# A hand-ordered first batch is reordered: thirteen exponential buffers, other engines for four casts, a split third hash, another beginning

## The chip, the cores and the metric

The kernel runs on one NeuronCore of a Trainium2 chip. The metric is the device time of one execution in microseconds (us); a lower time is better. One execution is also recorded by the hardware profiler, and its trace gives every instruction's start and length.

## The reference

Two blocks follow each other. Inputs are random normal: q, k, v of shape (4 batches, 8 heads, 768 rows, 64), a projection of 64 x 6, and the weights of a gated feed-forward block.

```python
q_bits = (einsum('bhsd,dk->bhsk', q, proj) > 0)        # 6 sign bits of each row; the same for k
mask   = q_bucket[:, :, :, None] == k_bucket[:, :, None, :]   # all six bits equal
scores = where(mask, q @ k.T / 8, -1e9);  attn = softmax(scores);  attn_out = attn @ v
x = attn_out.transpose(0, 2, 1, 3).reshape(3072, 512)
out = x + sigmoid(x @ w_res) * ((gelu(x @ w_gate) * (x @ w_val)) @ w_out)
```

So attention is restricted to rows that hash to the same of 64 buckets; then each of 3072 tokens goes through a feed-forward block of width 1536.

## The kernel before, in words

**Pairs and chunks.** Two heads make a pair p; a batch has four pairs, 0 to 3, and all four batches sixteen. For a pair, the rows of q (side 0) and k (side 1) lie on 128 partitions in 12 tiles of 128 rows (six of each head). The scores of a pair are cut into nine chunks of 1024 columns. Chunk c of the first batch (0 to 35, four pairs by nine) appears in the order as `('S', c)`: three matmuls into a PSUM tile `sp` (L500) of which there are two, and one exponential on ScalarE (ACT, L510) into a buffer. `('V', c)` is the product of that buffer with the values on TensorE (PE, L475).

**The hash as part of the scores.** A row carries, beside its 64 elements, six entries of plus or minus 0.5 from its sign bits and a constant, so that one matmul over 71 rows gives both the score and a large penalty where the bits differ. To get there: `cast` writes the elements as bf16 into `nat` (there are four `nat` tiles, pair p and side use number (2p+side) mod 4); `tr` transposes the f32 rows in 32x32 blocks on VectorE (DVE, L272) into `t32`; `hash` or `hash1` multiplies that with the projection on PE (L283, L318); `tokens` transposes the result back (L295); `bits` writes the signs (L304, L325); `turn` transposes `nat` on PE (L373) and `copy` takes it out of PSUM into `aug` (L381 on DVE, L379 on ACT), or `turn_dma` does both by a DMA on SP's queue (L360). The scores read `aug`.

**Values and results.** `va` and `vs` (GpSimd, POOL, L386 to L398) prepare the values and a sum over them; `finish` (DVE, L419 and L420) divides by the row sums into `x_tok`, which gets turned into `x_sb` by a DMA on SP's queue for pairs 0 and 1 (L428) and on PE for pairs 2 and 3 (`xturn`, L459, copied by L461 and L464). The feed-forward block of the first batch (L524, `gate_val`) reads `x_sb` and starts when the last pair's is there; before it, three quarters of its first two sums are done by `('gv', 0)` and `('gv', 1)`.

**Order.** Nothing is scheduled automatically: each engine runs its instructions in the order in which the code records them. For the first batch this is the list `PLAN`, entry by entry; `STEP` maps the names to functions. The letters in a step name the engine (`'v'` DVE, `'s'` ACT, `'p'` POOL). An entry's place binds only relative to others of its engine: a `load` is a DMA on SP's queue and is issued when the SP entries before it have been issued and its buffer is free. Buffers come free by use: q and k each have four load buffers, freed by `cast` and `tr` of the pair that held them. From batch 1 on, the order comes from loops that the change does not touch.

**Exponential buffers.** In the first batch the exponentials go round a ring of NE = 9 slots, which lies where `hidden` will be later; in later batches they go round the four buffers of `e_pool`.

Of the kernel before, what the change touches and what calls it, by code (L numbers as in the profile page):

```python
# [10 lines left out]
BF16 = mybir.dt.bfloat16  # L11
# [6 lines left out]
    ('load', 1, 0), ('load', 1, 1), ('load_v', 0), ('load', 2, 0), ('load_v', 1), ('load', 2, 1),  # L18
    ('load', 3, 0), ('proj', 's', 'pssp'), ('proj', 'w', 'pppp'), ('cast', 0, 1, 'p', 0, 6),
# [13 lines left out]
    ('S', 3), ('hash', (1,), 0), ('hash', (1,), 1), ('turn', 0, 1, 6, 12, 'f'), ('hash', (1,), 2),  # L33
    ('copy', 0, 1, 6, 8, 'v'), ('copy', 0, 1, 8, 12, 'v'), ('hash', (1,), 3),
# [5 lines left out]
    ('load', 4, 0),  # L40
    ('S', 8), ('V', 5), ('load_v', 4), ('turn', 1, 0, 6, 12, 'r'), ('copy', 1, 1, 0, 6, 'v'),
    ('finish', 0, 0),
    ('S', 9), ('V', 6), ('V', 7),
    ('S', 10), ('load', 5, 1), ('V', 8),
    ('S', 11), ('tr', 3, 1), ('tr', 2, 1), ('copy', 1, 0, 6, 12, 'v'), ('turn', 1, 1, 6, 12, 'f'),
    ('V', 9), ('finish', 0, 1),
    ('S', 12), ('hash', (2, 3), 0), ('hash', (2, 3), 1), ('va', 3), ('copy', 1, 1, 6, 12, 'v'),
    ('hash', (2, 3), 2), ('hash', (2, 3), 3), ('cast', 3, 1, 'p'),
# [7 lines left out]
    ('turn_dma', 3, 0),  # L56
# [15 lines left out]
    ('S', 34), ('hash', (4, 5), 0), ('finish', 3, 0), ('hash', (4, 5), 1),  # L72
    ('S', 35), ('V', 32), ('hash', (4, 5), 2), ('hash', (4, 5), 3), ('V', 33), ('va', 4),
    ('open', 4, 0), ('V', 34), ('V', 35), ('load', 7, 0), ('load_v', 6), ('tr', 7, 0), ('finish', 3, 1),
# [19 lines left out]
def kernel(  # L94
# [13 lines left out]
    B, H, S, D = q.shape  # L108
# [3 lines left out]
    P = 128  # L112
# [19 lines left out]
    NE = 9  # L132
# [108 lines left out]
    for s in range(3):  # L241
        n = KF // 3
# [166 lines left out]
    av = {}  # L409
# [383 lines left out]
```

## Time and profile before

| | |
|---|---|
| Time, median of 3 runs | 341.53 us (340.52 to 341.78) |
| Span of the profiled execution, first to last instruction | 338.4 us |
| The profiled execution's own time | not listed apart from its span; the median is 3.1 us above the span |
| PE, DVE, ACT, POOL busy | 330.2, 215.4, 214.3, 176.6 us |
| Granted TensorE clock, mean | 1.000 |
| DMA | 43.9 MB, mean 130 GB/s |

A row of the timeline gives the start, the length, the engine, the line of the kernel, the operation with what it writes and reads, and how many instructions are merged into it; in brackets stands how long the engine was idle before, and what ended that. "PEld" are weight loads of PE; an engine's name with a q is its queue. Matmuls are pipelined, so the rows of PE overlap.

### The profile page before, as it was taken

To read this page: it belongs to the slowest core of one execution; us is meant where nothing else is said; L and a number is where in the kernel's file an instruction comes from. 1 tells how busy PE (TensorE), PEld (TensorE's weight loads), DVE (VectorE), ACT (ScalarE), POOL (GpSimd) and SP (SyncE) were. 2 spreads that over 40 slices of the span, in tenths; PEclk is the share of its full clock that TensorE was granted. 3 is DMA by queue.
4 is the path that set the end of the run, shared out by engine and by line. 5 is a ranking of instruction groups with operands and counts; after the bars stand their busy time and mean duration, and the time that the engine had idled before them with its cause. 6 is when DMAs were issued, how large, how long until landed. Compare 5 with 4: busy or idle time off the path is not lost.

```text
span 338.4 us, 7607 instructions
## 1 busy us (share of the span) xinstructions
PE 330.2 (98%) x2995; PEld 203.2 (60%) x3042; DVE 215.4 (64%) x454; ACT 214.3 (63%) x247; POOL 176.6 (52%) x264
## 2 busy tenths in 40 slices
PE   8999999999999999999999999999999999999996
PEld 6676765565666655665666665666565665666444
DVE  7987465655477968877577896876478444343243
ACT  4989962237999962437999982255999984322220
POOL 3798930235289952578799981657979100000000
PEclk9999999999999999999999999999999999999999
DMA  6999999999966333529067932725050360000012
GB/s 216 371 259 177 289 191 152 166 161 227 300 207 158 82 97 82 96 44 188 3 157 231 280 90 85 141 47 93 2 125 33 79 103 31 33 0 2 31 62 97
DMA packets 74388, 43.89 MB, mean 130 GB/s; under 512 B 52544, under 2 KB 71360, under 8 KB 74352
## 3 DMA queue, kind: packets, MB, share of 16 engines
q1 hardware_dynamic: 67872, 37.95, 46.1%
q0 software_dynamic: 6400, 5.44, 10.5%
q8 instruction: 24, 0.39, 0.5%
q14 instruction: 12, 0.10, 0.1%
q10 hardware_dynamic: 80, 0.00, 0.0%
HBM read 29.56 MB, written 6.29 MB: 106 GB/s over the span
## 4 chain that ended last, share of the span: by engine, by line
PE 81%; POOL 8%; ACT 5%; DVE 3%; issue 2%; DMA 1%; POOLq 0%; DVEq 0%; ACTq 0%
PE sp L524 36%; PE fps L570 14%; PE sp L500 13%; PE av L475 7%; PE rps L556 5%; ACT ering L510 5%; POOL pr L335 4%; PE hs L283 3%; PE wps L228 1%; PE hs L318 1%; POOL v L394 1%; PE pt L373 1%; DMA x_sb<-x_tok 1%; DVE sums L341 1%; POOL va L386 1%
## 5 line engine op out<-in xcount | busy, mean ns | idle before, releaser
L335 POOL TENSOR_TENSOR pr<-ld,projr 128x384 f32<-128x384 f32 x96 | 93.8, 998 | 47.8 <-DVE sums L341 31.6
L510 ACT ACTIVATE e<-sp 128x1024 bf16<-128x1024 f32 x108 | 109.0, 1027 | 8.3 <-PE sp L500 3.2
L541 ACT ACTIVATE gt<-sp 128x768 bf16<-128x768 f32 x48 | 38.9, 810 | 82.3 <-PE sp L524 78.6
L500 PE MATMUL sp<-aug,aug 71*128 71x256 bf16 (+1 forms) x384 | 85.9, 325 | 1.2 <-ACT ering L510 0.6
L570 PE MATMUL fps<-wo,hh 128*128 128x512 bf16 (+2 forms) x287 | 74.4, 361 | 1.3
L544 DVE TENSOR_TENSOR hh<-gt,sp 128x768 bf16<-128x768 bf16 x48 | 45.8, 954 | 42.9 <-PE sp L524 39.1
L524 PE MATMUL sp<-x_sb,wg 128*128 128x512 bf16 (+1 forms) x377 | 70.5, 325 | 0.4
L524 PE MATMUL sp<-x_sb,wv 128*128 128x512 bf16 (+1 forms) x374 | 70.4, 324 | 0.5
L341 DVE TENSOR_REDUCE sums<-pr 128x6 f32<-128x384 f32 x96 | 50.2, 542 | 10.7 <-POOL pr L335 10.3
L475 PEld LDWEIGHTS <-e 128*128 128x128 bf16 x864 | 40.2, 97 | 25.1
L524 PEld LDWEIGHTS <-wg 128*128 128x128 bf16 x384 | 37.1, 98 | 25.8 <-issue 1.5
L524 PEld LDWEIGHTS <-wv 128*128 128x128 bf16 x384 | 37.5, 98 | 24.9 <-issue 0.2
L475 PE MATMUL av<-va,e 128*128 128x65 bf16 x864 | 43.4, 193 | 0.2
L570 PEld LDWEIGHTS <-hh 128*128 128x128 bf16 x312 | 28.1, 97 | 21.6
L500 PEld LDWEIGHTS <-aug 71*128 71x128 bf16 x384 | 29.3, 97 | 12.6 <-issue 3.7
L510 ACT ACTIVATE ering<-sp 128x1024 bf16<-128x1024 f32 x36 | 34.2, 1037 | 1.9 <-PE sp L500 1.7
L573 DVE SCALAR_TENSOR_TENSOR fps<-th,fps 128x512 f32<-128x512 f32 (+2 forms) x26 | 17.0, 653 | 25.9 <-PE fps L570 25.8
L556 PE MATMUL rps<-wr,x_sb 128*128 128x512 bf16 x91 | 26.0, 379 | 0.2
L560 ACT ACTIVATE th<-rps 128x512 f32<-128x512 f32 x24 | 14.3, 594 | 18.7 <-PE rps L556 18.5
L272 DVE STREAM_TRANSPOSE t<-ld 128x768 f32<-128x768 f32 (+3 forms) x28 | 23.1, 844 | 2.5 <-PE hs L283 1.9
L454 DVE COPY av<-av 128x390 f32<-128x390 f32 x24 | 13.6, 565 | 14.6 <-PE av L450 14.5
L262 POOL TENSOR_SCALAR nat<-ld 128x768 bf16<-128x768 f32 (+1 forms) x12 | 9.6, 804 | 19.9 <-DMA aug<-nat 16.9
(72 smaller groups left out, 264.4 us busy)
## 6 DMA issues: line engine op xcount, KB each, us to landing
ldv<-in_v_dram SPq DMA_DIRECT2D x16, 384.0 KB, 4.9
out_dram<-o SPq DMA_DIRECT2D x23, 256.0 KB, 2.1
ld<-in_q_dram SPq DMA_DIRECT2D x15, 384.0 KB, 5.1
ld<-in_k_dram SPq DMA_DIRECT2D x15, 384.0 KB, 5.2
wg<-in_moe_w_gate_dram POOLq DMA_DIRECT2D x4, 384.0 KB, 6.3
wv<-in_moe_w_val_dram POOLq DMA_DIRECT2D x4, 384.0 KB, 8.5
wo<-in_moe_w_out_dram POOLq DMA_DIRECT2D x3, 512.0 KB, 7.3
wr<-in_moe_w_res_dram POOLq DMA_DIRECT2D x1, 512.0 KB, 13.8
```

What stands on the lines that cost most here:

```text
L272: nc.vector.transpose(t32[p, side][:, sl].rearrange("p c h n -> p (c h n)"), raw[p, side][:, sl].rearrange("p c d -> p (c d)"))
L335: nc.gpsimd.tensor_mul(pr, raw[x][:, hi * T:(hi + 1) * T], projr[:, bit].unsqueeze(1).to_broadcast([P, T, D]))
L341: nc.vector.reduce_sum(sums[x][:, hi * T:(hi + 1) * T, bit], pr, axis=mybir.AxisListType.X)
L475: nc.tensor.matmul(av[p, hi][:, qt, :], e[:, off:off + P], va[:, hi, jt, 0:D + 1], start=first, stop=(repeats(p, hi) and jt == T - 1), ski ...
L500: nc.tensor.matmul(sp[:, off:off + nq * P], ks[0:KA, hi * T + jt, :], qs[0:KA, hi * T + qt0:hi * T + qt0 + nq, :], start=True, stop=True)
L510: nc.scalar.activation(e, sp, AF.Exp, scale=float(ALPHA))
L524: nc.tensor.matmul(sp[:, c0:c1], w[:, kk, bass.ts(m, P)], xs[:, kk, c0:c1], start=(kk == 0), stop=(kk == KM - 1))
L541: nc.scalar.activation(gt, sp[:, 0:S], AF.Gelu)
L544: nc.vector.tensor_mul(hidden[b][:, m, :], gt, ps[1][:, 0:S])
L556: nc.tensor.matmul(rps, x_sb[b][:, kk, t, :], wr[:, kk, :], start=(kk == 0), stop=(kk == KM - 1))
L570: nc.tensor.matmul(fps[:, cs], hh[:, m, bass.ts(t, P)], wo[:, m, cs], start=(m == 0), stop=(m == KF - 1))
L573: nc.vector.scalar_tensor_tensor(fps[:, cs], th[:, cs], 1.0, fps[:, cs], op0=ALU.add, op1=ALU.mult)
```

## The change

`PLAN` is replaced by another order of almost the same steps (36 S, 36 V, 20 `tr`, 14 `cast`, 15 `copy` in each), and the exponential of chunk c goes to slot c mod 13: slots 0 to 8 are the ring, and 9 to 12 are taken from `e_pool`. What else differs:

- `cast` of (2,1), (4,0), (4,1) and (5,0) is on DVE and no longer on POOL. Of the bits of pairs 2 and 3, DVE writes 11 parts of 16 (5 before).
- The third hash, `('hash', (4, 5), ...)`, has its four parts after chunks 29, 31 and 35 (two); before, after 34 (two) and 35 (two).
- At the beginning, POOL spreads the projection for the four-pair hash (`projw`) ahead of the one for the first pair (`projs`); the small 256-column filler matmul stands just before chunk 0; DVE's last transposition of the first q moves ahead of the first bits; four copies on ACT (three before) come ahead of chunk 0.
- The copy of (0,0) rows 6 to 12 goes from ACT to DVE, that of (0,1) rows 6 to 8 from DVE to ACT.
- The first two weight loads (`('w',)`) are issued on POOL behind `va` of pair 4 and not after chunks 6 and 13.
- SP issues the loads in another order: among them, `load` of (6,1) comes ahead of the first turn of x, and (5,1) behind it.
- The Gelu table is loaded ahead of the last copy of x.

The diff, cut to what the text speaks of:

```diff
-    ('load', 3, 0), ('proj', 's', 'pssp'), ('proj', 'w', 'pppp'), ('cast', 0, 1, 'p', 0, 6),
-    ('cast', 0, 0, 'p', 6, 12), ('tr', 0, 0, 0, 4), ('cast', 0, 0, 's', 0, 6), ('fill', 1, 256),
...
-    ('S', 10), ('load', 5, 1), ('V', 8),
...
-    ('V', 9), ('finish', 0, 1),
...
-    ('S', 15), ('load', 6, 1), ('bits', 3, 0, 'p'), ('V', 12), ('turn', 2, 1, 0, 6, 'f'),
...
-    ('S', 34), ('hash', (4, 5), 0), ('finish', 3, 0), ('hash', (4, 5), 1),
-    ('S', 35), ('V', 32), ('hash', (4, 5), 2), ('hash', (4, 5), 3), ('V', 33), ('va', 4),
+    ('proj', 'w', 'pppp'), ('tr', 0, 0, 0, 4), ('proj', 's', 'pssp'), ('cast', 0, 0, 'p', 6, 12),
+    ('tr', 0, 1, 0, 2), ('fill', 7), ('cast', 0, 0, 'p', 0, 6), ('hash1', 0, 0, 0, 4, 'av'),
+    ('load', 1, 0), ('tr', 0, 1, 2, 6), ('load', 1, 1), ('tr', 0, 0, 4, 6), ('hash1', 0, 1, 0, 2, 'av'),
+    ('cast', 0, 1, 'p', 6, 12), ('tr', 0, 0, 6, 12), ('bits1', 0, 1, 0, 2), ('cast', 0, 1, 's', 0, 6),
...
+    ('fill', 1, 256), ('tr', 1, 1), ('va', 0), ('load', 3, 1), ('load', 4, 0), ('copy', 0, 1, 2, 6, 's'),
+    ('copy', 0, 0, 4, 6, 's'),
+    ('S', 0), ('hash1', 0, 1, 6, 12, 'av'),
+    ('S', 1), ('turn', 0, 0, 6, 12, 'av'), ('bits1', 0, 1, 6, 12),
+    ('S', 2), ('hash', (1,), 2),
+    ('S', 3), ('turn', 0, 1, 6, 12, 'f'), ('hash', (1,), 3), ('copy', 0, 1, 6, 8, 's'), ('hash', (1,), 0),
+    ('vs', 0), ('cast', 2, 0, 'p'), ('tr', 2, 0), ('hash', (1,), 1), ('copy', 0, 0, 6, 12, 'v'),
+    ('tokens', (1,)),
...
+    ('S', 9), ('cast', 3, 0, 'p'), ('copy', 1, 0, 6, 12, 'v'), ('V', 6), ('load_v', 3), ('load', 6, 1),
+    ('S', 10), ('V', 7), ('vs', 1), ('tr', 3, 1), ('tr', 2, 1), ('turn', 1, 1, 6, 12, 'f'),
+    ('finish', 0, 0), ('V', 8), ('cast', 2, 1, 'v'),
+    ('S', 11),
+    ('S', 12), ('finish', 0, 1), ('hash', (2, 3), 0), ('hash', (2, 3), 1), ('hash', (2, 3), 2),
+    ('copy', 1, 1, 6, 12, 'v'), ('hash', (2, 3), 3), ('tokens', (2, 3)),
+    ('S', 13), ('bits', 2, 0, 'vvvp'), ('bits', 2, 1, 'vvvp'), ('V', 9), ('cast', 3, 1, 'p'),
...
+    ('S', 17), ('V', 14), ('copy', 2, 1, 0, 6, 'v'), ('load', 5, 1), ('copy', 2, 0, 0, 6, 'v'),
...
+    ('S', 19), ('va', 2), ('tr', 5, 1), ('copy', 2, 0, 6, 12, 'v'), ('finish', 1, 0), ('V', 15),
+    ('V', 16),
+    ('S', 20), ('copy', 2, 1, 6, 12, 'v'), ('V', 17), ('turn_dma', 3, 1),
...
+    ('S', 27), ('V', 24), ('tr', 5, 0), ('va', 4), ('V', 25), ('w',),
+    ('S', 28), ('V', 26),
+    ('S', 29), ('hash', (4, 5), 2), ('cast', 4, 1, 'v'), ('load_v', 6),
...
+    ('S', 31), ('finish', 2, 1), ('hash', (4, 5), 3),
...
+    ('S', 35), ('hash', (4, 5), 0), ('hash', (4, 5), 1), ('V', 33), ('V', 34), ('w',), ('tr', 7, 0),
+    ('V', 35), ('finish', 3, 1), ('gelu',), ('open', 4, 0), ('tr', 7, 1), ('gv', 0), ('vs', 4),
...
-            e = ring[0][:, (p * NCH + c) % NE]
+            n = (p * NCH + c) % (NE + 4)
+            e = ring[0][:, n] if n < NE else e_pool.tile([P, 1024], BF16, tag="e", name="e")
```

More of the change, by code (lines that the diff above doesn't have):

```diff
@@ L17 @@
 PLAN = [
-    ('load', 1, 0), ('load', 1, 1), ('load_v', 0), ('load', 2, 0), ('load_v', 1), ('load', 2, 1),
-    ('load', 3, 0), ('proj', 's', 'pssp'), ('proj', 'w', 'pppp'), ('cast', 0, 1, 'p', 0, 6),
[13 rows of a table removed]
-    ('S', 3), ('hash', (1,), 0), ('hash', (1,), 1), ('turn', 0, 1, 6, 12, 'f'), ('hash', (1,), 2),
-    ('copy', 0, 1, 6, 8, 'v'), ('copy', 0, 1, 8, 12, 'v'), ('hash', (1,), 3),
[5 rows of a table removed]
-    ('load', 4, 0),
-    ('S', 8), ('V', 5), ('load_v', 4), ('turn', 1, 0, 6, 12, 'r'), ('copy', 1, 1, 0, 6, 'v'),
-    ('finish', 0, 0),
@@ L43 @@
-    ('S', 9), ('V', 6), ('V', 7),
-    ('S', 10), ('load', 5, 1), ('V', 8),
-    ('S', 11), ('tr', 3, 1), ('tr', 2, 1), ('copy', 1, 0, 6, 12, 'v'), ('turn', 1, 1, 6, 12, 'f'),
-    ('V', 9), ('finish', 0, 1),
-    ('S', 12), ('hash', (2, 3), 0), ('hash', (2, 3), 1), ('va', 3), ('copy', 1, 1, 6, 12, 'v'),
-    ('hash', (2, 3), 2), ('hash', (2, 3), 3), ('cast', 3, 1, 'p'),
[7 rows of a table removed]
-    ('turn_dma', 3, 0),
[15 rows of a table removed]
-    ('S', 34), ('hash', (4, 5), 0), ('finish', 3, 0), ('hash', (4, 5), 1),
-    ('S', 35), ('V', 32), ('hash', (4, 5), 2), ('hash', (4, 5), 3), ('V', 33), ('va', 4),
@@ L74 @@
-    ('open', 4, 0), ('V', 34), ('V', 35), ('load', 7, 0), ('load_v', 6), ('tr', 7, 0), ('finish', 3, 1),
-    ('gv', 0), ('tr', 7, 1), ('xturn', 3), ('preset', 4, 0), ('tokens', (4, 5)), ('gv', 1),
-    ('repeat', 4, 0), ('gelu',),
+    ('proj', 'w', 'pppp'), ('tr', 0, 0, 0, 4), ('proj', 's', 'pssp'), ('cast', 0, 0, 'p', 6, 12),
[6 rows of a table added]
+    ('turn', 0, 1, 2, 6, 'f'), ('copy', 0, 0, 0, 4, 's'), ('load_v', 1), ('load', 3, 0),
+    ('bits1', 0, 0, 6, 12), ('tr', 1, 0), ('turn', 0, 0, 4, 6, 'r'), ('cast', 1, 0, 'p'),
@@ new lines @@
+    ('S', 12), ('finish', 0, 1), ('hash', (2, 3), 0), ('hash', (2, 3), 1), ('hash', (2, 3), 2),
+    ('copy', 1, 1, 6, 12, 'v'), ('hash', (2, 3), 3), ('tokens', (2, 3)),
+    ('S', 13), ('bits', 2, 0, 'vvvp'), ('bits', 2, 1, 'vvvp'), ('V', 9), ('cast', 3, 1, 'p'),
[17 rows of a table added]
+    ('S', 29), ('hash', (4, 5), 2), ('cast', 4, 1, 'v'), ('load_v', 6),
+    ('S', 30), ('V', 27), ('V', 28), ('tr', 6, 0), ('cast', 5, 0, 'v'),
+    ('S', 31), ('finish', 2, 1), ('hash', (4, 5), 3),
+    ('S', 32), ('V', 29), ('V', 30),
@@ L77 @@
+    ('S', 33), ('V', 31), ('finish', 3, 0), ('tr', 6, 1), ('load', 7, 1),
+    ('S', 34), ('V', 32), ('xturn', 2),
+    ('S', 35), ('hash', (4, 5), 0), ('hash', (4, 5), 1), ('V', 33), ('V', 34), ('w',), ('tr', 7, 0),
+    ('V', 35), ('finish', 3, 1), ('gelu',), ('open', 4, 0), ('tr', 7, 1), ('gv', 0), ('vs', 4),
+    ('xturn', 3), ('load_v', 5), ('preset', 4, 0), ('tokens', (4, 5)), ('repeat', 4, 0), ('gv', 1),
 ]
```

58 rows, old and new, of the table PLAN are left out of this document.

## The prediction, on record before the change was run

> **What bounds the kernel now.** I read the page first. Its chain of work that ended last gives PE most of the span, and the page's groups of instructions show that one exponential takes about a microsecond on ACT:
>
> ```profile
> PE 81%; POOL 8%; ACT 5%; DVE 3%; issue 2%; DMA 1%; POOLq 0%; DVEq 0%; ACTq 0%
> L510 ACT ACTIVATE ering<-sp 128x1024 bf16<-128x1024 f32 x36 | 34.2, 1037 | 1.9 <-PE sp L500 1.7
> ```
>
> The 81% is an average, and the change lies in the first batch alone. Everything behind it is the same program, bound by PE, so the change is worth exactly as much as it moves the start of the feed-forward block. ACT's timeline from 7 to 50 us shows what sets that start:
>
> ```profile
> 7.07 0.86 ACT L379 ACTIVATE aug<-pt 71x256 bf16<-71x256 bf16 x2 [1.04 <-PE pt L373]
> 8.42 0.38 ACT L379 ACTIVATE aug<-pt 71x256 bf16<-71x256 bf16 x1 [0.50 <-PE pt L373]
> 8.86 3.07 ACT L510 ACTIVATE ering<-sp 128x1024 bf16<-128x1024 f32 x3
> 11.83 0.80 ACT L379 ACTIVATE aug<-pt 71x768 bf16<-71x768 bf16 x1
> 12.52 1.02 ACT L510 ACTIVATE ering<-sp 128x1024 bf16<-128x1024 f32 x1
> 14.02 8.75 ACT L510 ACTIVATE ering<-sp 128x1024 bf16<-128x1024 f32 x9 [0.49 <-PE sp L500]
> 23.73 20.52 ACT L510 ACTIVATE ering<-sp 128x1024 bf16<-128x1024 f32 x22 [0.95 <-PE sp L500]
> 44.49 1.02 ACT L510 ACTIVATE ering<-sp 128x1024 bf16<-128x1024 f32 x1 [0.24 <-PE sp L500]
> 47.86 0.38 ACT L461 ACTIVATE x_sb<-pt 128x256 bf16<-128x256 bf16 x1 [2.35 <-PE av L450]
> ```
>
> The 36 exponentials run nearly without a break: chunk 0 at 8.86, chunk 3 at 12.52, 4 at 14.02, 13 at 23.73, 35 at 44.49. In the chain of waits between 30 and 34 us they are the chain itself, one behind the other:
>
> ```profile
> 31.28 0.80 ACT ering L510
> 32.19 0.81 ACT ering L510
> 33.09 0.82 ACT ering L510
> ```
>
> They start 0.90 to 0.91 apart; I take 0.915 as the free pace. From chunk 0 to 35 that would be 35 x 0.915 = 32.0 us; it took 35.63. So **3.6 us is all that any order can win** if chunk 0 stays where it is. The losses are at chunk 3 and 4 (5.16 - 4 x 0.915 = 1.5), at 5 to 13 (9.71 - 8.2 = 1.5), and little after. The 22 from chunk 13 pace at (20.52 - 1.02) / 21 = 0.929, which puts chunk 22 at 32.1.
>
> **The change, part by part.** I follow when chunks 0, 4, 13, 22 and 35 get their exponential.
>
> *Chunk 0.* Before, the beginning runs so:
>
> ```profile
> 1.07 3.38 PE L228 MATMUL wps<-warm 128*128 128x256 bf16 x8 [1.07 <-POOL warm L191]
> 3.12 0.43 POOL L222 COPY projs<-projn 32x12 f32<-32x12 f32 x2 [1.26 <-DMA projn<-in_proj_dram]
> 3.60 0.87 POOL L222 COPY projw<-projn 32x12 f32<-32x12 f32 x4
> 4.24 1.78 PE L318 MATMUL hs<-t,projs 128*128 128x128 f32 x8
> 5.34 0.33 DVE L323 STREAM_TRANSPOSE hs<-hs 128x128 f32<-128x128 f32 x1 [0.66 <-PE hs L318]
> 5.84 1.07 PE L318 MATMUL wps<-t,projs 128*128 128x128 f32 x8
> 6.45 0.57 DVE L272 STREAM_TRANSPOSE t<-ld 128x384 f32<-128x384 f32 x1
> ```
>
> With projw first, POOL gives projs at 3.12 + 0.87 + 0.43 and a gap, 4.47 for 3.55. The first hash then starts at about 4.7 for 4.24: 0.45 later. DVE's 0.57 of transposition (6.45) moves into its 0.66 of idle time ahead of 5.34 and would win that back, but DVE now takes the second hash's bits first and so waits for both; the turns end about 0.45 later. And ACT has four copies ahead of chunk 0: the new one has the 512 columns that the pair of 0.86 also holds next to a 256 (0.38), so some 0.5, less 0.2 of the 0.50 that ACT idled. Chunk 0: 8.86 + 0.45 + 0.3 = **9.6, 0.75 later**.
>
> *Chunk 4.* How long a chunk takes from the start of its scores on PE to its exponential, where ACT stands idle, chunk 13 shows (exponential at 23.73):
>
> ```profile
> 23.02 0.61 PE L500 MATMUL sp<-aug,aug 71*128 71x256 bf16 x3
> ```
>
> So 0.65 to 0.7. ACT's copy of 768 columns (0.80; it pushed chunk 3 to 12.52) goes to DVE, and a 256-column one (0.38) comes behind chunk 3. Chunks 1 to 3 then follow at the free pace, chunk 3 at 9.6 + 2.75 = 12.35; the copy ends at 13.7, and chunk 4 follows 0.65 later: **14.35, now 0.3 later** than before.
>
> *Chunk 13.* Here PE's whole second hash stood in the way before, and DVE's queue will after:
>
> ```profile
> 21.36 0.54 DVE L381 COPY aug<-pt 71x768 bf16<-71x768 bf16 x1
> 21.59 1.51 PE L283 MATMUL hs<-t,projw 128*32 128x192 f32 x32
> 23.16 0.58 DVE L295 STREAM_TRANSPOSE ht<-hs 128x384 f32<-128x384 f32 x1 [1.26 <-PE hs L283]
> 23.93 3.57 POOL L304 TENSOR_SCALAR nat<-ht 32x72 bf16<-32x72 f32 x7
> 27.87 0.82 POOL L264 CAST nat<-ld 128x768 bf16<-128x768 f32 x1 [0.37 <-POOL nat L304]
> 45.44 0.98 DVE L272 STREAM_TRANSPOSE t<-ld 128x768 f32<-128x768 f32 x1 [1.91 <-PE hs L283]
> ```
>
> The copy at 21.36 is the last that chunk 13 needs. DVE gets there without a pause, now with 0.5 more (the first hash of a whole pair ends later, behind chunk 3) and with the cast of (2,1). No cast on DVE is in the trace. It has 768 elements like the 71x768 copy (0.54) and f32 in SBUF like the transposition of 0.98; I take 0.54, the same operation. The copy ends at 21.9 + 0.5 + 0.54 = 22.95 (23.4 with 0.98), just after the hash (23.0); chunk 13 comes 0.65 later: **23.6, 0.1 earlier** (24.05, 0.3 later, with 0.98).
>
> *Chunk 22* needs two copies of pair 2, and DVE's queue holds `tr` of (5,1) and one `finish` ahead of them. Before, that load was issued at 21.16, long ahead. After, it is on SP behind the turn of x, and its buffer, pair 3's, comes free only with the cast of (3,1): 23.0 + 0.6 (transposition back) + 0.1 + 2 x 0.51 (POOL's bits, 3.57 / 7) + 0.82 = 25.6. How long it then takes, these issues tell: in order the turn of x, the loads issued at 21.16, 23.04, 32.52 and 33.95, and two half loads at the beginning:
>
> ```profile
> x_sb<-x_tok SPq DMA_TRANSPOSE x1, 5.9
> ld<-in_k_dram SPq DMA_DIRECT2D x1, 384.0 KB, 5.6
> ld<-in_k_dram SPq DMA_DIRECT2D x1, 384.0 KB, 8.1
> ld<-in_q_dram SPq DMA_DIRECT2D x1, 384.0 KB, 4.4
> ldv<-in_v_dram SPq DMA_DIRECT2D x1, 384.0 KB, 4.2
> ld<-in_q_dram SPq DMA_DIRECT2D x1, 192.0 KB, 2.4
> 29.42 2.68 DVE L272 STREAM_TRANSPOSE t<-ld 128x768 f32<-128x768 f32 x3
> 32.21 0.56 DVE L420 TENSOR_TENSOR x_tok<-av,rec 128x384 bf16<-128x384 f32 x1
> ```
>
> It has one transfer ahead of it and no weights beside it, so I take 4.2, the row nearest: landing at 29.8, between 28.0 (2.4, half the size, nothing ahead) and 33.7 (8.1). Behind the landing stand 0.9 (2.68 / 3), 0.54, 0.56 and a reciprocal of about 0.2, 0.54, and 0.65 to the exponential, less what neighbours overlap: 3.3. Chunk 22 comes at **33.1 for 32.1, 1.0 later**. At the free pace it would be due at 23.6 + 9 x 0.92 = 31.9, so the wait begins where the load lands after 28.6.
>
> *Chunk 35.* Half of the third hash stood between chunks 34 and 35 (44.49 - 43.23, if 21 paces of 0.929 lead from 23.73 to 43.23, is 1.26, so 0.35 lost); after, the parts lie where PE has room, two behind chunk 35. From 22 to 35: 13 x 0.915 + 0.1 = 12.0 for 12.4. Chunk 35: 33.1 + 12.0 = **45.1, 0.6 later**.
>
> *Behind it* nothing shortens. `tr` of (7,0) waited for the hash at 45.44 and stood ahead of the last `finish`, and does again. The earlier Gelu table saves what the four hash parts beside the first sums cover anyway.
>
> **Priced at nothing.** The thirteen buffers and the allowed lag: by the list, never more than six chunks are issued and not yet multiplied, before (at chunks 5 and 24) and after (at chunk 5), and nine slots hold six; no exponential waits for a slot in either. Three more casts and six more bits on DVE fall where it has pauses (28 to 36 us). The two weight loads issued late:
>
> ```profile
> 40.20 0.84 POOL L247 DMA_DIRECT2D wg<-in_moe_w_gate_dram  x1
> 46.27 1.14 PE L524 MATMUL sp<-x_sb,wg 128*128 128x512 bf16 x6
> wg<-in_moe_w_gate_dram POOLq DMA_DIRECT2D x4, 384.0 KB, 6.3
> ```
>
> They leave POOL behind `va` of pair 4, some three microseconds of casts earlier than 40.2 stood, say 38.5, and land at 44.8, 1.5 ahead of the first use at 46.27. If pair 4's values come two microseconds late, that cover is gone and each one more costs one.
>
> The sum: +0.75 - 0.45 - 0.4 + 1.1 - 0.4 = +0.6 on a span of 338.4, and so on the median of 341.53, which lies 3.1 above the span: **342.1**. A difference of 0.5% (1.7 us) is about what a measurement of this kernel can tell from no change.
>
> [...] POOL's cast takes 0.82 us here and never ran beside a cast on DVE. [...]
>
> **The rivals.**
>
> *The load of (5,1) comes much later (slower; 0.20).* One mechanism: DVE waits at `tr` of (5,1), and what stands behind it are the copies that chunk 22 reads. For it speaks the 8.1 of a load behind a turn of x; against it, that this one shared the DMA engines with a weight load that is moved away. From 31.3 on (5.6) it costs 1.5 more than forecast, at 33.7 it costs 3.9: 343.6 to 346.0.
>
> *PE's slow beginning lasts longer (slower; 0.10).* The eight matmuls of 4.24 took 1.78 us, the eight of the same shapes at 5.84 took 1.07: PE gets faster at about 5.9, after 4.8 us without a pause. After the change it idles between 4.1 and 4.7. If the faster stretch comes only at 9, the hash and turns ahead of chunk 0 cost up to 1.5 more: 343.6. [...]
>
> *The reorder works as such a plan would want (faster; 0.17).* The start is not later than before, since POOL's and ACT's copies overlap better than I let them (-0.75), the load lands by 28.6 (-1.1), and the cast costs less: 340.2, down to 339.5 where PE also closes the gap at chunk 13. Against it speaks that every one of these must hold.
>
> *It does nothing that can be told (forecast's own kind; 0.48).* Between +1.6 and -0.7: 340.8 to 343.1. The rest, 0.05, is weights or values late at 46 us, 344.
>
> **How the numbers follow.** Faster by over 0.5% (below 339.8): most of the faster rival's lower half and a little of its middle, 0.12. Slower by over 0.5% (above 343.2): 0.17 of the load, 0.08 of PE's beginning, 0.04 of the rest, 0.03 of the forecast's upper end, 0.32. Within: 0.56. The range goes from 340.0 (0.13 below it) to 344.6 (the load landing at 32.3; 0.07 above).
>
> **What would show it.** In the changed kernel's ACT timeline, chunk 0 near 9.6, 4 near 14.2, 13 near 23.6, 22 near 33.1 and 35 near 45.1. On DVE, an idle time ended by the DMA of a k load ahead of a transposition near 29 us, with chunk 22's scores waiting behind it. No wait of an exponential for PE's values. The forecast is wrong if chunk 35 starts outside 43.0 to 46.7, or if the distance from chunk 35 to the feed-forward block is not the same as before.

## The result, and the profile after

The changed kernel takes 346.05 us (343.90 to 348.35, six runs) against 340.81 (340.52 to 341.78, six runs of the kernel before on the same chip): 1.0146 times as long, 95% interval 1.0107 to 1.0185. The forecast was 342.1, with a range up to 344.6: the change is slower by more than the range held. The forecast stood on a median of 341.53 and meant 0.6 us more; measured are 5.2 more. (Ratios here leave disturbed executions out, so a ratio can be smaller than the quotient of the medians beside it.)

The profiled execution took 344.31 us, one of the faster of the six, with a span of 342.6 for 338.4. (The kernels' line numbers differ by a few.) The page's chain that ended last now has DMA in it with 6%, where it had 1%:

```profile
PE 78%; POOL 9%; DMA 6%; issue 3%; DVE 3%; ACT 0%; SPq 0%; POOLq 0%; DVEq 0%; ACTq 0%
```

ACT's timeline, in the rows that answer to those of before:

```profile
9.23 3.84 ACT L508 ACTIVATE ering<-sp 128x1024 bf16<-128x1024 f32 x4
12.95 0.38 ACT L376 ACTIVATE aug<-pt 71x256 bf16<-71x256 bf16 x1
13.96 4.83 ACT L508 ACTIVATE ering<-sp 128x1024 bf16<-128x1024 f32 x5 [0.63 <-PE sp L497]
23.50 8.60 ACT L508 ACTIVATE ering<-sp 128x1024 bf16<-128x1024 f32 x9 [0.60 <-PE sp L497]
31.98 3.85 ACT L508 ACTIVATE e<-sp 128x1024 bf16<-128x1024 f32 x4
44.12 1.02 ACT L508 ACTIVATE e<-sp 128x1024 bf16<-128x1024 f32 x1
49.72 0.38 ACT L458 ACTIVATE x_sb<-pt 128x256 bf16<-128x256 bf16 x1 [3.06 <-PE av L447]
```

Up to chunk 35 the change won 0.37 us (44.12 for 44.49). The 36 chunks are not where the time went. POOL's timeline behind them, and PE's first products of x with the weights, show where:

```profile
37.19 0.83 POOL L383 CAST va<-ldv 128x768 bf16<-128x768 f32 x1 [1.49 <-DMA ldv<-in_v_dram]
37.95 0.15 POOL L384 MEMSET va<- 128x12 bf16 x1
42.67 0.99 POOL L244 DMA_DIRECT2D wg<-in_moe_w_gate_dram  x1 [4.57 <-issue]
43.67 0.75 POOL L244 DMA_DIRECT2D wv<-in_moe_w_val_dram  x1
48.20 1.15 PE L522 MATMUL sp<-x_sb,wg 128*128 128x512 bf16 x6 [2.38 <-DMA wg<-in_moe_w_gate_dram]
50.20 1.15 PE L522 MATMUL sp<-x_sb,wv 128*128 128x512 bf16 x5 [0.49 <-DMA wv<-in_moe_w_val_dram]
```

POOL is done with pair 4's values at 38.1, the weight load stands next in its program with no wait of its own, and it leaves 4.57 us later ("issue": nothing that the profile shows was waited for). It lands at 48.16, the second one at 50.16, and PE waits for both. The first exponential of the second batch, chunk 36, stands behind all this; its row before, then after:

```profile
80.74 1.02 ACT L510 ACTIVATE e<-sp 128x1024 bf16<-128x1024 f32 x1
83.19 1.02 ACT L508 ACTIVATE e<-sp 128x1024 bf16<-128x1024 f32 x1
```

It comes **2.44 later**, with chunk 35 0.37 earlier. A second loss of **1.65** follows between chunks 48 and 64 of the second batch (20.05 us for 18.40); from there the distance of 4.1 us stays, and the span ends 4.2 later.

### The profile page after: what moved, and what is told of

It reads as the page before. It is cut to its first block, busy times and chain, and to the rows that moved or that the text cites. A ratio compares the mean times of both kernels' runs of the same rounds, so it can differ in the third digit from the quotient of the medians.

```text
span 342.6 us, 7607 instructions
## 1 busy us (share of the span) xinstructions
PE 330.5 (96%) x2995; PEld 202.0 (59%) x3042; DVE 219.0 (64%) x463; ACT 214.2 (63%) x247; POOL 172.4 (50%) x255
## 4 chain that ended last, share of the span: by engine, by line
PE 78%; POOL 9%; DMA 6%; issue 3%; DVE 3%; ACT 0%; SPq 0%; POOLq 0%; DVEq 0%; ACTq 0%
PE sp L522 36%; PE fps L568 14%; PE sp L497 12%; PE av L472 6%; PE rps L554 5%; POOL pr L332 3%; PE hs L280 2%; DMA wv<-in_moe_w_val_dram 2%; POOL va L383 1%; DMA ld<-in_q_dram 1%; DMA ldv<-in_v_dram 1%; POOL v L391 1%; PE pt L370 1%; PE hs L315 1%; DMA x_sb<-x_tok 1%
## 5 line engine op out<-in xcount | busy, mean ns | idle before, releaser
L508 ACT ACTIVATE e<-sp 128x1024 bf16<-128x1024 f32 x117 | 117.9, 1026 | 10.0 <-PE sp L497 4.8
L472 PEld LDWEIGHTS <-e 128*128 128x128 bf16 x936 | 43.4, 97 | 26.6 <-issue 0.7
L472 PE MATMUL av<-va,e 128*128 128x65 bf16 x936 | 47.0, 193 | 0.2
L508 ACT ACTIVATE ering<-sp 128x1024 bf16<-128x1024 f32 x27 | 25.7, 1026 | 1.3 <-PE sp L497 1.2
L417 DVE TENSOR_TENSOR x_tok<-av,rec 128x384 bf16<-128x384 f32 x32 | 17.8, 557 | 1.1
```

The lines of the kernel that those rows point to most:

```text
L417: nc.vector.tensor_mul(x_tok[b][:, hp, :, hi * D:(hi + 1) * D], o[:, 0:T, 0:D], rec.unsqueeze(2).to_broadcast([P, T, D]))
L472: nc.tensor.matmul(av[p, hi][:, qt, :], e[:, off:off + P], va[:, hi, jt, 0:D + 1], start=first, stop=(repeats(p, hi) and jt == T - 1), ski ...
L508: nc.scalar.activation(e, sp, AF.Exp, scale=float(ALPHA))
```

## What the experiments showed

Theory at the start: the two late weight loads are the whole loss. Rivals: the second batch's loss has another cause; the pause of 4.57 us comes from the new DVE casts beside it, or from transfers in flight, or from POOL's instruction stream. In the diffs, "..." marks lines that are left out, and some lines are cut at their ends.

### 1. The weights early again (e1_w_early)

```diff
-    ('S', 6), ('turn', 1, 0, 0, 6, 'r')
+    ('S', 6), ('w',), ('turn', 1, 0, 0, 6, 'r')
...
-    ('S', 13), ('bits', 2, 0, 'vvvp'), ('bits', 2, 1, 'vvvp'), ('V', 9), ('cast', 3, 1, 'p'),
+    ('S', 13), ('bits', 2, 0, 'vvvp'), ('bits', 2, 1, 'vvvp'), ('V', 9), ('cast', 3, 1, 'p'), ('w',),
...
-    ('S', 27), ('V', 24), ('tr', 5, 0), ('va', 4), ('V', 25), ('w',),
+    ('S', 27), ('V', 24), ('tr', 5, 0), ('va', 4), ('V', 25),
...
-    ('V', 34), ('w',), ('tr', 7, 0),
+    ('V', 34), ('tr', 7, 0),
```

> The changed kernel with its first two weight loads back at chunks 6 and 13, where the kernel before has them; everything else as changed. Theory W (the late weights are the whole loss; 2.44 us at the first product of x with the gate weights, and 1.65 more between chunks 48 and 64 as a consequence of the same lateness): chunk 35 stays near 44.1, chunk 36 comes near 80.4 for 83.2, the 1.65 us behind chunk 48 go too, and the time is 340.4 (340.0 to 341.0). Rival R (the 1.65 us in the second batch have a cause of their own, such as the ring's buffers): 342.1. Rival N (the first products are late for another reason and the weights only show as what came last): 345 to 346.

341.84 us (340.66 to 343.85, ten runs), ratio 1.0043 [1.0018, 1.0068]. Chunk 36 at 80.86 for 83.19: the first loss is the weights'. But 1.3 of the second loss stayed, and the median lies 1.4 above theory W: the late loads are not the whole loss. And chunk 35 came at 44.86, since the second load, issued at 25.32, puts POOL's later work back, and the values of pair 2 are ready 0.7 later, for which PE now waits:

```profile
32.77 0.40 PE L472 MATMUL av<-va,ering 128*128 128x65 bf16 x8 [1.15 <-POOL va L384]
```

### 2. The kernel before with late weights (e2_before_w_late)

```diff
-    ('S', 6), ('w',), ('bits', 1, 1, 'v'),
+    ('S', 6), ('bits', 1, 1, 'v'),
-    ('S', 13), ('cast', 3, 0, 'p'), ('w',), ('tokens', (2, 3)),
+    ('S', 13), ('cast', 3, 0, 'p'), ('tokens', (2, 3)),
-    ('V', 33), ('va', 4),
+    ('V', 33), ('va', 4), ('w',), ('w',),
```

> The kernel before with only its first two weight loads moved from chunks 6 and 13 to behind the values of pair 4 at chunk 35; nothing else changed. Theory W1 (being issued late costs it by itself, since POOL stands idle for some 4.5 us ahead of the first weight load of the group, as in the changed kernel): loads leave at 42 to 43, land at 48, first use about 2 us late, and the other weights later too: 343 to 346. Rival W2 (the 4.5 us of idle time belong to the changed kernel's other transfers, not to the late place): the loads leave at 38.4, land by 43.6 and 45.6, the first use at 46.3 is not late, time 340.8 to 341.8.

342.1 us (340.99 to 345.51, ten runs), 1.0051 [1.0015, 1.0087]. There is no pause, though the loads stand in the same place, right behind the values of pair 4, and are the first that POOL issues:

```profile
40.47 0.16 POOL L387 MEMSET va<- 128x12 bf16 x1
40.51 0.98 POOL L247 DMA_DIRECT2D wg<-in_moe_w_gate_dram  x1
```

They land at 46.22 and 48.14, and the first product comes at 46.58 for 46.27. So late issue alone costs little in this execution, the second fastest of the ten; what makes the 4.57 us is not the late place by itself, which speaks for W2, though the loads left 2 us later than W2 said and the median lies 0.3 above its range. Three of the ten runs, at 344.6 to 345.5, stay unexplained.

### 3. Nine buffers (e3_ring9)

```diff
-            n = (p * NCH + c) % (NE + 4)
-            e = ring[0][:, n] if n < NE else e_pool.tile(...)
+            e = ring[0][:, (p * NCH + c) % NE]
```

> The changed kernel with nine exponential buffers in a ring as before in place of thirteen; the lists stay as changed. Theory: the thirteen buffers do nothing (at most six chunks wait for their values), so the time stays at that of the changed kernel, 346 (344 to 348.5). Rival: the four buffers that it takes from the pool of the later batches, or their order, cost the 1.65 us in the second batch: 344.4 or less. Second rival: the buffers are needed and without them an exponential waits for values: above 348.

346.11 us (345.01 to 346.67, four runs), 1.0152 [1.0120, 1.0185]: the thirteen buffers make no difference that can be told. The pause is there too, 4.82 us, up to 43.01.

This profile shows one more cost of PE's wait. PE waits 2.69 us for the first weight load, and from 49.5 to 52.8 the clock that it is granted is 0.50, where the changed kernel's profile has 1.00. The same six transpositions of x, here (first row) and in the changed kernel:

```profile
49.49 0.85 PE L456 MATMUL pt<-ident,x_tok 128*128 128x128 bf16 x6
49.19 0.50 PE L456 MATMUL pt<-ident,x_tok 128*128 128x128 bf16 x6
```

Chunk 36 comes at 84.59 for 83.19, though the load landed only 0.3 later. In the profile of experiment 6 the clock is 0.50 from 48.4 to 55.1, behind a wait of 1.90; no other profile of these kernels has it below 1.00 before its last 3 us. By these figures such a stretch takes some 1.6 us of PE's work (an estimate: half of 3.3). It fits the runs: the mean granted clock is 0.992 to 0.995 in four of the changed kernel's six, and no run of the kernel before beside the experiments is under 0.997. That the wait brings the lower clock on was not tested by itself.

### 4. The loads a few instructions earlier (e4_w_ahead)

Beside this, the two late places are taken out as in experiment 1.

```diff
-    ('load_v', 4), ('vs', 3),
+    ('load_v', 4), ('vs', 3), ('w',), ('w',),
```

> The changed kernel with its first two weight loads only a few instructions earlier on POOL: behind the sums of pair 3 (about 33.9 us) instead of behind the values of pair 4 (38.1 us). Theory F (POOL's 4.57 us of idle time at 38.1 is a refill of its instruction stream, queued behind loads in flight; it comes at a fixed place in the stream and time, whatever instruction stands there): both loads leave at 34 to 36 without a pause, land by 42, and the pause shows behind them, at the next instructions near 38 to 42: time 340.4 to 342. Theory S (the pause belongs to the first transfer that POOL issues): the pause of some 4.5 us stands ahead of the first weight load, at 34 to 38.5, landing near 44 and 46, and nothing pauses at 38 to 42 afterwards: time 341 to 343. Theory W in either case: faster than the changed kernel by 3 us or more.

346.24 us (342.16 to 347.66, four runs), 1.0116 [1.0051, 1.0182]: no theory held. POOL pauses nowhere: the first load leaves at 35.97, at once, and nothing stops at the place of the old pause, behind the values of pair 4.

```profile
35.93 0.11 POOL L395 MEMSET vsum<- 128x2 bf16 x1
35.97 0.99 POOL L244 DMA_DIRECT2D wg<-in_moe_w_gate_dram  x1
39.47 0.16 POOL L384 MEMSET va<- 128x12 bf16 x1
39.54 1.35 POOL L391 TENSOR_TENSOR v<-ldv 128x384 f32<-128x384 f32 x1
```

But now the weights are among the loads of 34 to 40 us. The first weight load takes 9.1 us and the second 12.6, and the k load of pair 7 lands at 51.41 for 42.38, for which DVE waits with the copy of x behind it:

```profile
51.43 0.98 DVE L269 STREAM_TRANSPOSE t<-ld 128x768 f32<-128x768 f32 x1 [2.24 <-DMA ld<-in_k_dram]
52.77 0.48 PE L522 MATMUL sp<-x_sb,wg 128*128 128x512 bf16 x2 [2.04 <-DVE x_sb L459]
```

The wait was turned into another one. This execution also began 2 us late, chunk 0 at 11.28; more of that below.

### 5. The casts by themselves (e5_port)

A kernel of stretches that begin with an ACT copy; in each, POOL casts and then issues two weight loads, and DVE does what the expectation lists.

> A kernel that leaves out the whole computation and writes zeros. It measures, one stretch behind the other, two weight loads issued by POOL behind a cast of POOL's, with beside them: A nothing; B one cast by VectorE (128x768, f32 to bf16, both in SBUF) that begins as POOL's cast ends; C that cast, a transposition, a scaling cast and a copy from PSUM, as in the changed kernel; D three transpositions; E six casts; F one cast, then VectorE idle for 3 us and a transposition; G three copies from PSUM; H two casts with almost nothing on POOL ahead; I five loads in flight; J five loads in flight and VectorE as in C. Theory P (a cast by VectorE beside it holds up the issue of a POOL load): A, D, G, I issue the first load within 0.2 us of POOL's cast; B, C, E, F, H, J show 0.5 us (the length of the cast) to 5 us (as in the changed kernel) more; if the pause ends only with VectorE's next instruction, F is 3 us longer than B. Theory F (the pause comes from loads in flight, in whose queue something waits that POOL needs): only I and J show a pause of 2 us or more, and I as much as J.

No stretch shows a pause. POOL's rows of A (alone), E (six casts beside it), J (at least five loads in flight, and DVE as in the changed kernel), and DVE's of E:

```profile
9.46 0.82 POOL L73 CAST pc<-go 128x768 bf16<-128x768 f32 x1 [9.02 <-ACT go L62]
10.22 1.62 POOL L70 DMA_DIRECT2D w<-in_moe_w_gate_dram  x2
37.93 0.83 POOL L73 CAST pc<-go 128x768 bf16<-128x768 f32 x1 [4.88 <-ACT go L62]
38.69 1.51 POOL L70 DMA_DIRECT2D w<-in_moe_w_gate_dram  x2
77.61 0.82 POOL L73 CAST pc<-go 128x768 bf16<-128x768 f32 x1 [5.11 <-ACT go L62]
78.38 1.51 POOL L70 DMA_DIRECT2D w<-in_moe_w_gate_dram  x2
38.13 3.86 DVE L76 CAST vc<-go 128x768 bf16<-128x768 f32 x6
```

With six casts beside it the first load landed after 5.30 us, alone after 5.42. In J it landed after 10.53, but it left as promptly. Neither DVE's casts nor loads in flight held up the issue here: in all three stretches the first load leaves 0.76 to 0.77 us after the start of POOL's cast.

### 6. The two casts back on POOL (e6_casts_back)

```diff
-    ('S', 29), ('hash', (4, 5), 2), ('cast', 4, 1, 'v'), ('load_v', 6),
-    ('S', 30), ('V', 27), ('V', 28), ('tr', 6, 0), ('cast', 5, 0, 'v'),
+    ('S', 29), ('hash', (4, 5), 2), ('cast', 4, 1, 'p'), ('load_v', 6),
+    ('S', 30), ('V', 27), ('V', 28), ('tr', 6, 0), ('cast', 5, 0, 'p'),
```

> The changed kernel with the casts of (4,1) and (5,0) on POOL as before instead of VectorE; the weight loads stay late. Theory P (VectorE's cast beside it holds up the first late load): no pause at 38.1 us, the first load leaves by 38.3 and lands by 43.5, the second leaves near 40.6 and lands near 46; chunk 36 at 80.3 to 81.2 for 83.19; time 341.0 to 343.0. Theory F (a refill or a queue behind the loads in flight): the pause of 4 to 5 us stays, chunk 36 at 83 or later, time 346 or more, since POOL also has 1.6 us more to do.

348.05 us (345.53 to 348.98, four runs), 1.0203 [1.0170, 1.0236]. DVE has no cast there, and the pause stays:

```profile
37.81 0.15 POOL L384 MEMSET va<- 128x12 bf16 x1
42.06 0.99 POOL L244 DMA_DIRECT2D wg<-in_moe_w_gate_dram  x1 [4.11 <-PE sp L497]
```

Theory P is refuted. (The releaser that the row names belongs to the cast behind it, whose wait POOL's sequencer reached just before.) The trace adds a hint: POOL's sequencer, which can take the waits of later instructions while earlier ones run (11 of its 45 separate waits in the changed kernel's trace, up to 0.77 us ahead), reached the next one, that of the cast, only at 42.05. By this it was the stream that stood.

What comes just before the pause's end is in the packet records. Beside the loads there are packets of 8 KB on a queue of the kind "instruction". In the changed kernel the part of the DMA view for 40.5 to 41.2 us has one (columns: packets, MB, share), the view for 38.2 to 40.6 none:

```profile
q14 instruction: 1, 0.01, 3.1%
```

The starts of this packet and of the first weight load:

| kernel | packet starts | load starts | difference |
|---|---|---|---|
| changed | 40.76 | 42.67 | 1.91 |
| 3, nine buffers | 41.05 | 43.01 | 1.96 |
| 6, casts back | 40.18 | 42.06 | 1.88 |
| 10, eight fills (below) | 40.90 | 42.70 | 1.80 |

(A second such packet comes at 41.4 to 42.7 in these. It goes with ACT's count of instructions: when it starts, ACT has 67 to 71 recorded instructions behind it in every kernel, 69 before (at 40.83) and 69 in the changed one (at 42.27). In 3 the two packets lie 0.4 us apart, and the table takes the first. Measured from the packet's end instead, the difference is 1.5 to 1.6; the expectation of experiment 8 says "started" for that.) In the kernels without a pause the packet comes at 31.21 (before), 30.33 (experiment 2), 38.56 (experiment 1) and 42.67 (experiment 4, where POOL had by then gone on beyond that place for 4 us and had its first transfer long behind it).

### 7. The loads where POOL idles (e7_w_gaps)

The two late places are taken out as in experiment 1.

```diff
-    ('S', 6), ('turn', 1, 0, 0, 6, 'r')
+    ('S', 6), ('w',), ('turn', 1, 0, 0, 6, 'r')
...
-    ('S', 10), ('V', 7), ('vs', 1),
+    ('S', 10), ('V', 7), ('vs', 1), ('w',),
```

> The changed kernel with the first weight load at chunk 6 and the second at chunk 10, behind the sums of pair 1, where POOL waits for 2.6 us anyway (in the first experiment the second one, at chunk 13, made the values of pair 2 late, and PE waited 1.15 us for them). Theory: chunk 23 follows 22 without the pause, chunk 35 stays at 44.1, chunk 36 comes at 80.1 to 80.4 (before: 80.74), and the time is 340.2, 0.4 below the kernel before; with the second batch's loads also as early as before. Rival 1 (the second weight load shares the transfers with the load of (5,1), which lands 2 to 3 us later and holds up chunk 22): 341.5 to 342.5. Rival 2 (the second batch loses 1 to 1.5 us as in the first experiment whatever chunk 35 does, since its turns and output weights fall on each other): 341.5.

341.88 us (339.56 to 343.24, twelve runs), 1.0017 [0.9997, 1.0038]: the loss is gone, but the 340.2 of the theory was reached by the lower group of runs alone: five lie at 339.6 to 340.8 and seven at 341.8 to 343.2. The profiled one, 343.24, is of the upper group, and both of its delays stand in the prediction as rivals. DVE waits for the load of (5,1), which shares the transfers with a weight load, and chunk 22 follows chunk 13 0.8 us later than in the changed kernel:

```profile
31.79 0.98 DVE L269 STREAM_TRANSPOSE t<-ld 128x768 f32<-128x768 f32 x1 [2.42 <-DMA ld<-in_k_dram]
```

And PE stays slow: chunk 0 comes at 11.38. PE's first hashes, of this kernel (first two rows) and of experiment 1 (last two), whose beginning is the same program:

```profile
4.56 1.97 PE L315 MATMUL hs<-t,projs 128*128 128x128 f32 x8 [0.33 <-POOL projs L219]
6.33 1.92 PE L315 MATMUL wps<-t,projs 128*128 128x128 f32 x8
4.68 1.10 PE L315 MATMUL hs<-t,projs 128*128 128x128 f32 x8 [0.44 <-DVE t L269]
5.62 1.06 PE L315 MATMUL wps<-t,projs 128*128 128x128 f32 x8
```

In three of the eight profiles with this beginning (4, 7, 8) PE runs at about half speed up to some 10.2 us (1.91 to 1.97 us for eight hashes that take 1.06 to 1.10 when it is fast) and chunk 0 comes at 11.3 to 11.4; in five at 9.0 to 9.2. The runs of experiments 1 and 9, too, lie in two groups.

### 8. A small first transfer (e8_small_first), and 9. Twelve more instructions (e9_more_pool)

```diff
-    ('S', 7), ('V', 4), ('va', 1),
+    ('S', 7), ('V', 4), ('va', 1), ('tiny',),
```

where `tiny` is, in 8 and in 9:

```python
nc.gpsimd.dma_start(little, moe_w_gate[0:P, 0:16])

for i in range(12):
    nc.gpsimd.memset(little[:, i:i + 1], 0.0)
```

> The changed kernel with one very small extra transfer (128 x 16 numbers that nothing reads) issued by POOL at chunk 7, where POOL has time; the weight loads stay late. In the three kernels that pause ahead of the first weight load (the changed one, the one with nine buffers, the one with the casts back), the load begins 1.55 to 1.6 us after an 8 KB instruction packet of queue 14 has started to land (40.76, 41.05, 40.18, and loads at 42.67, 43.01, 42.06). Theory R1 (the first transfer that POOL ever issues cannot go while POOL's instructions are being refilled, later ones can): no pause at 38.1, first load leaves by 38.5; chunk 36 at 80.3 to 81.3; time 2 to 4 us below the changed kernel, 341 to 343.5. Theory R2 (whatever stands at that place of POOL's stream waits for the refill): the pause stays, 4 us, perhaps one instruction earlier; time as the changed kernel, 344 to 348.

> The changed kernel with twelve very small sets (128 x 1) on POOL at chunk 7, where it idles 1.6 us; nothing else. They move every later instruction of POOL twelve places down its stream, so the refill is asked for about 8 us earlier, before the loads of 33 to 37 us are in the transfer queues. Theories R1 and R2 (the pause is the refill's): the 8 KB packet lands near 31 to 35 us instead of 40.8, no pause ahead of the first weight load, which leaves by 38.5; chunk 36 at 80.3 to 81.3, time 341 to 343.5. Theory N (the pause has nothing to do with where POOL is in its stream): the pause of 4 us stays, 344 to 348.

8: 342.81 us (340.37 to 344.20, ten runs), 1.0047 [1.0027, 1.0068]. 9: 343.23 us (340.71 to 344.88, ten runs), 1.0050 [1.0022, 1.0078]. The weight loads stand at the same late place as in the changed kernel, and neither pauses (all of 8's execution is 2 us late, by PE's slow beginning); POOL's rows of 8, then of 9:

```profile
39.50 0.15 POOL L389 MEMSET va<- 128x12 bf16 x1
39.55 0.85 POOL L249 DMA_DIRECT2D wg<-in_moe_w_gate_dram  x1
38.55 0.14 POOL L390 MEMSET va<- 128x12 bf16 x1
38.59 0.99 POOL L250 DMA_DIRECT2D wg<-in_moe_w_gate_dram  x1
```

In 9 the packet comes at 28.79 for 40.76 and nothing else was done, so by its time and its queue's kind ("instruction") the packet is taken as a refill of POOL's instructions, and the pause belongs to where POOL stands in its stream. In 8 the packet starts at 39.42 and the load at 39.55, with no 1.9 us between: a transfer that is not POOL's first did not wait for it. So R1 fits every profile: **POOL's first transfer, met by an outstanding refill of POOL's instructions, waited for it** (it left 1.80 to 1.96 us behind the packet's start in four profiles); ordinary instructions (experiment 4) and later transfers (8) did not. The part on later transfers rests on 8's one profile, and whether 4's refill, at 42.67, was asked for when its first load left, no row shows. Why the first transfer waited was not found. That the refill was late because the loads of 33.5 to 37.2 us, which took 4.4 to 6.3, were in the transfer queues is likely from experiment 9, where it came before them; no run took those loads away.

Experiment 9 also prices lateness without the pause: loads leave at 38.59, as forecast, but land at 46.45 and 48.37, PE waits 0.70 and 0.41, and chunk 36 follows 35 after 37.30 us for 36.26.

### 10. Eight fills (e10_fill8), 11. with the weights mended too (e11_gaps_fill8)

```diff
-    ('tr', 0, 1, 0, 2), ('fill', 7),
+    ('tr', 0, 1, 0, 2), ('fill', 8),
```

> The changed kernel with eight instead of seven filling products on TensorE ahead of the first hash, so that TensorE does not idle from 4.23 to 4.6 us. In two of six profiled kernels with the new beginning the first hashes ran at half speed up to 10.3 us (eight matmuls in 1.97 us instead of 1.10) and chunk 0 came at 11.3 instead of 9.1. Theory C (the pause at 4.2 lets the clock's slow beginning last longer in about half of the executions): the runs no longer fall in two groups 2.2 us apart; the changed kernel's upper ones (347.6, 348.4) go, median about 344.3 for 346.05. Rival (the two groups come from somewhere else): the spread of over 3 us stays, median 345.5 to 346.5.

> The changed kernel with both of its faults mended: weight loads at chunks 6 and 10 (as in the seventh experiment) and eight filling products. Theory: every run near the lower group of the seventh experiment, 339.6 to 340.8, median 340.1; chunk 0 at 9.1, chunk 35 at 44.1 to 44.6, chunk 36 at 80.4; 0.5 us below the kernel before, about the least that can be told. Rival (the second batch's turns and output weights still fall on each other in some executions): 340.8 to 342.

10: 344.21 us (342.67 to 346.56, six runs), 1.0106 [1.0073, 1.0138]; the median is that of theory C, but a spread of 3.9 us stayed and the interval overlaps that of the changed kernel, so this alone decides nothing. 11: 341.31 us (340.25 to 350.51, twelve runs), 1.0025 [0.9999, 1.0051], nine runs at 340.25 to 341.49 and three at 344.2 and above. In both profiles PE gets fast between 5.9 and 6.4, and chunk 0 comes at 9.73 and 9.51: not the long slow beginning, but 0.3 to 0.7 us behind the fast case. The 340.1 of 11's theory was not reached. Its three upper runs have a mean granted clock of 0.995, 0.995 and 0.976, the other nine 0.997 to 1.000; why was not found.

### 12. The old order of the two projections (e12_projs_first)

The edit is made in the kernel of experiment 7.

```diff
-    ('proj', 'w', 'pppp'), ('tr', 0, 0, 0, 4), ('proj', 's', 'pssp'),
+    ('proj', 's', 'pssp'), ('tr', 0, 0, 0, 4), ('proj', 'w', 'pppp'),
```

> The kernel of the seventh experiment (weight loads at chunks 6 and 10, seven fills) with the two copies of the projection in their old order: projs ahead of projw, so that POOL has projs ready near 3.6 us instead of 4.5. Theory C (the gap ahead of the first hash is what lets the slow beginning of TensorE last): the first hash follows the fills at 4.2 to 4.4, chunk 0 at 8.6 to 9.1 in every execution, chunk 35 at 43.5 to 44.2, chunk 36 at 79.6 to 80.3, time 339.4 to 340.2, no group of runs 2.2 us higher; faster than the kernel before by 0.6 to 1.2 us. Rival 1 (the first hash waits for VectorE's transposition, which ends at 4.64 in the profiles of the new beginning, as much as for projs): the gap of 0.4 us stays, and the two groups of runs stay as in the seventh experiment, median 341 to 342.

340.28 us (339.90 to 341.02, twelve runs), 0.9989 [0.9978, 1.0000]. The upper group of experiment 7 is gone. PE's first hash follows the fills with no gap and at full speed; ACT's rows behind it:

```profile
4.00 1.08 PE L315 MATMUL hs<-t,projs 128*128 128x128 f32 x8
8.88 3.84 ACT L508 ACTIVATE ering<-sp 128x1024 bf16<-128x1024 f32 x4
43.70 1.02 ACT L508 ACTIVATE e<-sp 128x1024 bf16<-128x1024 f32 x1
48.25 0.81 ACT L539 ACTIVATE gt<-sp 128x768 bf16<-128x768 f32 x1 [1.03 <-PE sp L522]
```

Rival 1 fell: where projs was early, the transposition held nothing up. (Full speed from the first hash on is one profile's. Those of before, 2, 10 and 11 have no gap either; there PE got fast at 5.8 to 6.8, never as late as 10.2.) This is the change with its two faults taken out: chunk 35 0.79 and chunk 36 1.02 earlier than before (79.72). The time is 0.1% lower, just short of the least gain expected, 0.6 us, and at the edge of what its interval can tell. Of the 1.02 us the profiled span shows 0.35, because the part behind chunk 108 took 101.12 us for the 100.46 of the profile of before; it took 101.0 to 101.5 in all twelve experiments but the fifth, also in the second, which has the old list, and 100.60 in the changed kernel. What makes it shorter in those two profiles stays open.

## Why the second batch lost 1.65

SP's turns of pairs 4 to 7 and the output weights fall on each other in the queues, later and for longer than before, and behind them stand the q loads of the second batch, with which POOL begins its hash products. The eight turns take SP from 60.83 to 91.87 us for 58.39 to 84.07, the output weights leave at 68.8 to 77.4 for 64.9 to 71.3 and take 8.3 us in the median for 7.3, and the first of the q loads is issued at 91.92 for 84.12. Late weights are one way into this, but neither needed nor enough: in experiment 1, with the first two loads early, the product was nearly as late, and in 2, with them late, nothing was lost. POOL's row of the first product, before and after:

```profile
88.89 1.95 POOL L335 TENSOR_TENSOR pr<-ld,projr 128x384 f32<-128x384 f32 x2 [4.78 <-DMA ld<-in_q_dram]
96.28 2.90 POOL L332 TENSOR_TENSOR pr<-ld,projr 128x384 f32<-128x384 f32 x3 [4.36 <-DMA ld<-in_q_dram]
```

How long behind chunk 36 that product came, and how much longer than 18.39 us chunks 48 to 64 took, in twelve profiles:

| kernel | product behind chunk 36 | loss, chunks 48 to 64 |
|---|---|---|
| 11, before, 7, 9, 2 | 8.00, 8.15, 8.30, 10.31, 11.39 | 0.00 to 0.01 |
| 3, 8 | 11.89, 11.94 | 0.45, 0.49 |
| 4, 10 | 12.23, 12.55 | 0.78, 1.10 |
| 1, changed | 12.78, 13.09 | 1.32, 1.66 |
| 6 | 14.14 | 2.44 |

Up to 11.4 us nothing is lost, and beyond it each microsecond costs about 0.9 (from 11.89 to 14.14, 1.99 lost for 2.25; from 11.89 to 12.78, 0.87 for 0.89). So POOL's products had at least 3.2 us to spare before. In the waits of PE from 90 to 118 us, where before has none, it shows only in small pieces, 0.8 of the 1.65 in all (columns: us in total, times, longest):

```profile
PE fps L568 <- DVE o L574: 0.4, 1, 0.4
PE av L447 <- POOL pr L332: 0.2, 1, 0.2
PE av L447 <- DVE av L439: 0.2, 1, 0.2
```

That the lateness is the cause is read from this table; no kernel moved the product alone.

## Why the prediction was wrong

- **The step that failed is "Priced at nothing ... the two weight loads issued late"**. "Leave POOL ... say 38.5": they left at 42.67 and 43.67, the pause, which no row of before could show, since there POOL's first transfer was long past. Only the first load was priced: the second lands 2.0 later and is waited for as well. The flight of 6.3 us was not too short here (5.5), but without the pause it would have been: then the two took 7.9 and 8.8 (experiment 9), in the same transfers as four other loads. What the prediction said of the cover, 1.5 us, "each one more costs one", was right, and so was the place to look: the distance from chunk 35 to the feed-forward block, which it named as what would make it wrong (from chunk 35 to 36 it is 39.1 us for 36.3). This case lay in "the rest", with 0.05 and 344.
- **"The change is worth exactly as much as it moves the start of the feed-forward block"** failed too. The block's first product came 1.9 later, chunk 36 behind it 2.4, and the span is 4.2 longer: what was late in the queues outlived the point where PE becomes the bound. And the median went up by 5.2, where the profile has 4.2; the lower granted clock of experiment 3 and PE's slow beginning, of which this profile has neither, would make up the rest, which no profile of a slower run shows.
- **Chunk 0**: 9.6 forecast, 9.23 in the profile, 11.3 in three of the other seven profiles of this beginning. The rival "PE's slow beginning lasts longer" (0.10) named it; its 1.5 us is 2.1 to 2.3, as the faster stretch comes at 10.2 and not 9. It is likely a part of why six runs spread over 4.4 us. That the cause is projw ahead of projs, experiment 12 says with twelve runs and one profile. The length of PE's idle time ahead of the hashes does not decide it alone: experiment 7's profile idled 0.33 us there and stayed slow to 10.2, the changed kernel's own idled 0.31 and got fast near 5.4 (its first eight hashes took 1.47 us), experiment 6's idled 0.51 and was fast at once (1.10), and experiment 12's, with no idle time, was fast from its first hash at 4.00, 2.9 us after PE's first product. What sets the moment was not found.
- **Chunk 4**: 14.35 forecast, 13.96. **Chunk 13**: 23.6, 23.50; DVE's cast of (2,1), priced at 0.54, took 0.55.
- **Chunk 22**: 33.1 forecast, 31.98. The load of (5,1) was put at 25.6, behind the cast of (3,1). It was issued at 23.68, right behind the turn of x, while that cast ran only at 24.74: it did not wait for that buffer. It then took 3.6 for 4.2, landed at 27.25, and DVE did not wait. The rival of 0.20 is real, as experiment 7 shows, but did not come about here.
- **Chunk 35**: 45.1 forecast, 44.12. The reorder won more than was granted, and chunks 0 to 35 take 34.9 us for 35.6.
- **The thirteen buffers** make no difference that can be told (experiment 3), as said.
- **DVE's casts beside POOL's work**, of which before has none: DVE's cast of (4,1) took 1.09 beside POOL's cast, for 0.55 alone, and POOL's sum of the values 1.35 for 1.00 beside DVE's casts (experiment 1). So each took longer beside the other, which the sum left out; the price fell where little waited.

## What to carry to other kernels

A load that has idle time to be issued in is not free to be issued late, as experiment 9 shows (chunk 36 follows 35 1.0 us later): there the two loads took 7.9 and 8.8 us among four others, where before one took 6.3 in the median, and POOL's first product of the second batch came 10.31 us behind chunk 36 for 8.15. Price its landing with the loads in flight then, the second transfer as well as the first, and follow the queue past the first consumer to the next one with little slack. And give a pause ahead of TensorE's first real work a price of its own, since it can cost in some executions what a single profile need not show (here chunk 0 at 11.3 to 11.4 for 9.0 to 9.2 us in three of eight profiles).

## What had not been expected of the hardware

- POOL's first transfer of a run began 1.8 to 2.0 us behind the start of an 8 KB packet of instructions whenever the two met, and POOL stood for 4.1 to 4.8 us (four profiles). Twelve small instructions ahead, or one small transfer, removed it. Ordinary instructions at that place went on in experiment 4: the sum of pair 4's values began at 39.54, right behind the values, with the packet at 42.67.
- The same eight matmuls took 1.10 to 1.47 us or 1.97 at the same place of the same beginning, and two more rows of hashes with the 1.97 were slow as well, in different executions.
- In two profiles (experiments 3 and 6) PE's granted clock was 0.50 for 3.3 and 6.7 us behind waits of 2.69 and 1.90 us; in others (changed, 4, 10), waits of 2.0 to 2.4 left it at 1.00.
